# Zero-padded attention rows, more filler matmuls and separate PSUM banks in a fused pooled-attention and soft-MoE kernel

## The chip, the core and the metric

The kernel runs on one core of a Trainium2 chip. The time is what the device takes for one launch, in microseconds (us). It was measured in three runs: median 175.56 us, lowest 175.49, highest 175.78. A profiled execution of the same kernel gives the views that are quoted below. Its engines are PE (matmuls; PEld is the load of their stationary operand), DVE (vector), ACT (scalar), POOL (GpSimd, which here issues the loads) and SP (which issues the stores).

## The reference

Two stages are computed. The first is attention with keys and values that are means over eight neighbouring positions; the second mixes all tokens into 32 slots, runs four slots through each of eight experts, and mixes the slots back into the tokens.

```python
# batch 8, heads 8, seq 576, head_dim 64; pool = 8, so 72 keys and values
k_p = k.reshape(B, H, Sp, pool, D).mean(axis=3)
v_p = v.reshape(B, H, Sp, pool, D).mean(axis=3)
attn = softmax(scale * q @ k_p.T)
x = (attn @ v_p).transpose(0, 2, 1, 3).reshape(4608, 512)
logits = x @ phi                              # 4608 x 32
d = softmax(logits, axis=0)                   # over the tokens
slot_input = d.T @ x                          # 32 x 512, four rows for each expert
h = maximum(slot_input[e] @ w1[e], 0)         # 512 -> 1024, eight experts
slot_out[e] = h @ w2[e]                       # 1024 -> 512
c = softmax(logits, axis=1)                   # over the slots
out = c @ slot_out                            # 4608 x 512, float32
```

Inputs and outputs are float32. The kernel works in bf16; the loads convert on the way.

## The kernel before, in words

Batches are taken two at a time: four pairs. Within a pair there are two quarters `qd`, of four heads each and both batches. For each pair `prepare_kq` (L248) averages k by matmuls with `pmat` (L227), turns the means over (L243) and turns q over (L259). `prepare_v` (L270) does the same for v and multiplies by `iphi`, so that each row of `vp` holds 64 values of v and the 32 values of v times phi. A column of ones in `vp` (L154) makes the sum of the exponentials.

`score_unit` (L294) forms scores for one head: two matmuls with 64 contracted rows (L299) and one ACT exponential (L301) into `exa`, of which 72 partitions are used, one for each pooled key. `u_tile` (L304) takes the exponentials as the stationary operand and `vp` as the moving one (L314), 128 tokens at a time. DVE then takes the reciprocal of the sums (L319, tile `rec`, three buffers) and scales the result into `xs` (L325), or ACT does the scaling (L323). One quarter has nine u tiles; tiles 4 to 8 of a quarter are formed while the next quarter's scores are computed. Those of the very last quarter come behind the loop, in part in PSUM that the scores used (`spare`).

`combine` (L376) takes a finished pair: `weigh` (L328) sums the logits over the heads, on PE by default and for pair 1 on POOL (`ADDERS`), and exponentiates them to `ee`; `gather` (L346) multiplies `ee` with x into `G_ps`; `turn` (L358) turns `ee` over into `cT`. For the last pair this is written out behind the loop.

Then come the experts: `hidden` (L521) for the first layer, `second_layer` (L545) for the second, `row_sums` and `turn_sums` (L414, L423) for the sums of c. The last expert's second-layer weights arrive in two halves of columns, three pieces each (L499), in memory that the last pair frees late. `begin` (L622) starts the output of one half, and `tiles` and the last loop write the rest, 36 row tiles in all, stored by SP (L607).

`busy(n)` (L583) is a filler: a float32 matmul of n columns on data in `cT`, whose result nobody reads. A scheduler orders the instructions of PE, ACT, DVE and SP up to the end of the attention part; POOL's order is as written throughout, and behind the attention part the order of all engines is as written. Each engine runs its own row in that order, and waits on semaphores where an operand is not ready. The loads all go through one queue that POOL issues to, and they land in the order of issue.

Of the kernel before, what the change touches and what calls it, by code (L numbers as in the profile page):

```python
# [8 lines left out]
FP = mybir.dt.float32  # L9
BF = mybir.dt.bfloat16  # L10
# [8 lines left out]
def kernel(  # L19
# [10 lines left out]
    nc = tc.nc  # L30

    B, H, S, D = q.shape
    POOL = 8
    SP = S // POOL
# [15 lines left out]
    XW = D + NS  # L50
    HQ = H // 2
# [98 lines left out]
    nc.scalar.copy(out=big[:, 0, CUT // 2:CUT], in_=kf[:, CUT // 2:CUT])  # L150

    vp = [consts.tile([SP, H, XW + 2], BF, name=f"vp{i}") for i in range(5)]
    for t in vp:
        nc.vector.memset(t[:, :, XW:XW + 1], 1.0)  # L154
# [115 lines left out]
    def prepare_v(pair):  # L270
# [13 lines left out]
        for b in range(2):  # L284
            for qd in range(2):
                ps = ps_m.tile([SP, HQ, XW], FP, name="v_ps", tag="m")
                for hh in range(0, HQ, 2):
                    n = (qd * HQ + hh) // 2
                    nc.tensor.matmul(out=ps[:, hh:hh + 2], lhsT=vpar[:, b * HQ + n], rhs=iphi[:, n],
                                     start=True, stop=True)  # L290
                nc.scalar.copy(out=vp[(2 * pair + b) % 5][:, qd * HQ:(qd + 1) * HQ, 0:XW], in_=ps)
                yield
# [11 lines left out]
    def u_tile(pair, qd, t, ex, by_scalar=False, ps=None):  # L304
# [13 lines left out]
        rec = small.tile([128, HQ], FP, name="rec", bufs=3)  # L318
# [55 lines left out]
    ADDERS = {1: 2}  # L374
# [75 lines left out]
    last = None  # L450
    for pair in range(NP):
        for qd in range(2):
# [4 lines left out]
            ex = [exa[0:SP, (2 * pair + qd) % 2, b] for b in range(2)]  # L457
            for i in range(9):
                if i < 8:
                    score_unit(pair, i // 4 * H + qd * HQ + i % 4, ex[i // 4][:, i % 4])  # L460
# [120 lines left out]
    cTf = cT.rearrange("p r u -> p (r u)").bitcast(FP)  # L581

    def busy(n):  # L583
        nc.tensor.matmul(out=idle[:, 0:n], lhsT=cTf[:, 0:128], rhs=cTf[:, 0:n], start=True, stop=True)
# [80 lines left out]
    busy(512)  # L665
    turn_sums()
    busy(512)
    busy(512)
    for e in range(4, E - 2):
        second_layer(e)  # L670
    busy(512)
    second_layer(E - 2, 0, 5)
    busy(512)
    second_layer(E - 2, 5, FJ)
    second_layer(E - 1, 0, 3, 0)
    second_layer(E - 1, 3, J7, 0)
# [43 lines left out]
```

## Time and profile before

| what | value |
|---|---|
| runs: median, lowest, highest | 175.56, 175.49, 175.78 us |
| the profiled execution's own time | 175.54 us |
| its span, first to last instruction | 173.8 us |
| mean granted TensorE clock | 0.916 |
| busy: PE, DVE, ACT, POOL | 128.0, 93.0, 89.1, 21.7 us |
| loads through POOL's queue | 30.48 MB written, 85.5% of 16 DMA engines' span |
| stores and one load through SP's queue | 10.49 MB, 15.3% |
| loads last issued, at 138.71 us; first store issued | 147.31 us |

The profile gives the stretch, engine and line of each instruction. In a row of the order in time the first number is the start in us from the span's start, the second the length; in square brackets stands the idle time of the engine just before and what ended it. In a row of a stretch each engine's busy time is followed by its instructions in brackets; then come the granted clock (1.00 is full speed), the share of the 16 DMA engines, and GB/s. In a row of a group the number ahead of the bar is its busy time and the mean in ns. "72*128" ahead of a shape means 72 contracted rows and 128 columns of the stationary operand.

### The profile page before, as it was taken

Reading aid. Unit: us, or ns where it says so; the run is one execution under the profiler, and the core shown is the slowest. Engines: PE = TensorE matmul, PEld = TensorE weight load, DVE = VectorE, ACT = ScalarE, POOL = GpSimd, SP = SyncE. Lnnn points to the kernel's source line nnn. Section 1 sums busy time; section 2 is a strip of 40 time slices with the busy share of each in tenths; the row PEclk is TensorE's granted clock in tenths of the full one; section 3 lists DMA queues with packets and bytes.
Section 4 is the critical chain, followed back from the end, with each engine's and each line's share of the span. In section 5 each row is a group of like instructions: output and inputs, shape, how many; then the busy total and the mean of one; then the engine's idle time right before and its main releaser. Section 6 shows DMA issues by size and latency. Waiting matters only on the chain.

```text
span 173.8 us, 2847 instructions
## 1 busy us (share of the span) xinstructions
PE 128.0 (74%) x1104; PEld 69.0 (40%) x1104; DVE 93.0 (54%) x255; ACT 89.1 (51%) x171; POOL 21.7 (12%) x37
## 2 busy tenths in 40 slices
PE   0005787999899999999699999637999995897000
PEld 0002443665555665556444665422453322432000
DVE  5403344397868589786972856750542002799000
ACT  3201249885887739888490895463021103898000
POOL 7000111022100040009000104001410000000000
PEclk9999999999999999999957999955799999999555
DMA  5999999999999999999999999999999999999994
GB/s 192 247 216 223 216 216 212 220 214 212 218 218 214 215 219 214 218 215 214 215 219 211 223 211 219 213 221 211 223 211 219 208 197 177 301 390 447 404 453 183
DMA packets 8989, 41.13 MB, mean 237 GB/s; under 512 B 640, under 2 KB 4736, under 8 KB 5136
## 3 DMA queue, kind: packets, MB, share of 16 engines
q0 software_dynamic: 6080, 30.48, 85.5%
q1 hardware_dynamic: 2896, 10.49, 15.3%
q8 instruction: 8, 0.13, 0.3%
q14 instruction: 5, 0.04, 0.1%
HBM read 61.93 MB, written 9.44 MB: 411 GB/s over the span
## 4 chain that ended last, share of the span: by engine, by line
PE 40%; DMA 20%; ACT 16%; DVE 11%; issue 4%; POOL 1%; DVEq 0%; ACTq 0%; POOLq 0%
DMA xsa<-in_moe_w_dram 14%; PE pool_ps L227 9%; ACT exa L301 7%; DMA phi_f<-in_moe_phi_dram 7%; PE u_ps L314 6%; PE sc L299 6%; PE G_ps L349 4%; PE q_ps L259 4%; DVE w_sb L590 4%; DVE xsa L325 4%; PE lg_ps L342 2%; PE turn_ps L243 2%; ACT vmeans L233 2%; DVE rec L319 2%; PE f_ps L611 2%
## 5 line engine op out<-in xcount | busy, mean ns | idle before, releaser
L301 ACT ACTIVATE exa<-sc 72x576 bf16<-72x576 f32 x64 | 39.3, 653 | 6.6 <-PE u_ps L314 3.4
L325 DVE TENSOR_TENSOR xsa<-u_ps,rec 128x384 bf16<-128x384 f32 x66 | 35.8, 553 | 1.2
L314 PE MATMUL u_ps<-vp,exa 72*128 72x97 bf16 (+1 forms) x304 | 25.0, 215 | 4.6 <-DVE xsa L325 3.6
L314 PEld LDWEIGHTS <-exa 72*128 72x128 bf16 (+1 forms) x320 | 17.7, 103 | 15.6 <-DVE xsa L325 6.1
L299 PE MATMUL sc<-qTa,kp 64*72 64x288 bf16 x128 | 22.0, 313 | 1.6 <-ACT exa L301 1.0
L227 PE MATMUL pool_ps<-big,pmat 128*128 128x512 bf16 x64 | 17.5, 398 | 0.7 <-ACT qTa L263 0.6
L319 DVE RECIPROCAL rec<-u_ps 128x4 f32<-128x4 f32 x69 | 11.2, 174 | 11.5 <-PE u_ps L314 11.2
L179 PE MATMUL phi_ps<-spread,sel 128*128 128x256 bf16 x4 | 1.3, 394 | 15.1 <-DVE spread L174 15.1
L349 PE MATMUL G_ps<-xsa,ee 128*128 128x512 bf16 x36 | 11.5, 481 | 1.2 <-ACT ee L343 1.2
L259 PE MATMUL q_ps<-ident,big 128*128 128x128 bf16 x144 | 11.6, 219 | 0.8 <-DVE qTa L265 0.2
L299 PEld LDWEIGHTS <-kp 64*72 64x72 bf16 x128 | 7.9, 109 | 8.4 <-issue 3.0
L235 DVE TENSOR_REDUCE rsum<-rest_ps 128x64 f32<-128x512 f32 x8 | 5.5, 692 | 9.6 <-PE rest_ps L231 9.6
L265 DVE COPY qTa<-q_ps 128x768 bf16<-128x768 bf16 x16 | 8.7, 552 | 3.1 <-PE q_ps L259 3.0
L611 PE MATMUL f_ps<-so,cT 128*128 128x512 bf16 (+1 forms) x36 | 9.6, 353 | 0.7 <-ACT w_sb L588 0.6
L259 PEld LDWEIGHTS <-big 128*128 128x128 bf16 x144 | 8.6, 97 | 3.3 <-issue 1.8
L590 DVE TENSOR_SCALAR w_sb<-f_ps,recR 128x512 f32<-128x512 f32 x14 | 9.3, 741 | 0.1
L263 ACT COPY qTa<-q_ps 128x768 bf16<-128x768 bf16 x8 | 6.4, 795 | 5.7 <-PE q_ps L259 5.7
L590 DVE TENSOR_SCALAR exa<-f_ps,recR 128x256 f32<-128x256 f32 x8 | 3.8, 483 | 9.9 <-PE f_ps L633 9.6
L233 ACT CAST vmeans<-pool_ps 128x1024 bf16<-128x1024 f32 x4 | 4.0, 1012 | 9.2 <-PE pool_ps L227 9.2
L227 PEld LDWEIGHTS <-pmat 128*128 128x128 bf16 x64 | 5.9, 101 | 6.8 <-issue 2.1
L588 ACT ACTIVATE w_sb<-f_ps,recR 128x512 f32<-128x512 f32 x14 | 8.4, 696 | 0.2
L499 POOL DMA_DIRECT2D xsa<-in_moe_w_dram x6 | 4.1, 695 | 27.4 <-PE G_ps L349 13.2
(109 smaller groups left out, 160.9 us busy)
## 6 DMA issues: line engine op xcount, KB each, us to landing
w_sb<-in_moe_w_dram POOLq DMA_DIRECT2D x2, 3072.0 KB, 38.3
big<-in_q_dram POOLq DMA_DIRECT2D x4, 1152.0 KB, 12.8
big<-in_v_dram POOLq DMA_DIRECT2D x4, 1152.0 KB, 16.7
big<-in_moe_w_dram POOLq DMA_DIRECT2D x1, 4096.0 KB, 32.3
big<-in_k_dram POOLq DMA_DIRECT2D x3, 1152.0 KB, 21.4
out_dram<-w_sb SPq DMA_DIRECT2D x1, 3072.0 KB, 10.9
w_sb<-in_moe_w_dram POOLq DMA_DIRECT2D x2, 1024.0 KB, 19.6
qTa<-in_moe_w_dram POOLq DMA_DIRECT2D x1, 2048.0 KB, 33.2
```

Of the source, the lines that this page charges most:

```text
L227: nc.tensor.matmul(out=ps, lhsT=pmat, rhs=src[:, t:full * POOL:POOL, :], start=(t == 0), stop=(t == POOL - 1))
L259: nc.tensor.transpose(out=ps[:, t].rearrange("p n i -> p (n i)"), in_=q_sb[pair][:, tt:tt + 2, :].rearrange("p t d -> p (t d)"), identity= ...
L265: nc.vector.tensor_copy(out=dst, in_=ps)
L299: nc.tensor.matmul(out=ps[:, r, 0:S // 2], lhsT=kp[pair][rows, n], rhs=qT[pair][rows, n].rearrange("p t i -> p (t i)"), start=True, stop=True)
L301: nc.scalar.activation(out=dst.rearrange("p r (i t) -> p r i t", t=NU), in_=ps[:, :, 0:S // 2].rearrange("p r (t i) -> p r i t", i=NI), fu ...
L314: nc.tensor.matmul(out=ps[rows, hh], lhsT=ex[b][:, hh].rearrange("p r t -> p (r t)")[:, c:c + rows.stop - rows.start], rhs=vp[(2 * pair + ...
L319: nc.vector.reciprocal(out=rec, in_=ps[:, :, XW])
L325: nc.vector.tensor_tensor(out=dst, in0=ps[:, :, 0:XW], in1=rec.rearrange("p h -> p h ()").to_broadcast([128, HQ, XW]), op=ALU.mult)
L349: nc.tensor.matmul(out=ps, lhsT=ee[:, t].rearrange("p g s -> p (g s)"), rhs=x[:, t, :, 0:D], start=(t == 0), stop=(t == 8))
L588: nc.scalar.activation(out=dst, in_=src, func=AF.Copy, scale=by)
L590: nc.vector.tensor_scalar(out=dst, in0=src, scalar1=by, scalar2=None, op0=ALU.mult)
L611: nc.tensor.matmul(out=ps, lhsT=tokens(n), rhs=so[:, cols], start=True, stop=True)
```

## The change

Six things change.

- The tiles `vp` get 128 partitions instead of 72 and are zeroed by DVE first; partitions 64 to 127 of `exa` are zeroed too, once at the start. The u matmuls then contract 128 rows, 56 of them zero. The exponentials and the values are written to the first 72 as before.
- `rec` has eight buffers instead of three.
- Pair 0's logits are summed by DVE (`ADDERS` 0: 1), in one reduction over the heads, instead of by eight matmuls.
- Of the five last u tiles, those with i = 1 and 2 use the two `sc` tiles, one bank each; before, i = 2, 3 and 4 used three banks of them.
- Four fillers are added behind the last scores: 256 columns behind u tiles 1 and 4, 512 behind the logits, 256 behind the gather.
- In the expert part one more filler of 512 columns stands behind the row sums, and one of 256 ahead of each of the last expert's first two groups of slices.

```diff
+    nc.vector.memset(exa[64:128].rearrange("p n b h r t -> p (n b h r t)").bitcast(FP), 0.0)
-    vp = [consts.tile([SP, H, XW + 2], BF, name=f"vp{i}") for i in range(5)]
+    vp = [consts.tile([128, H, XW + 2], BF, name=f"vp{i}") for i in range(5)]
     for t in vp:
+        nc.vector.memset(t, 0.0)
         nc.vector.memset(t[:, :, XW:XW + 1], 1.0)
...
-        rec = small.tile([128, HQ], FP, name="rec", bufs=3)
+        rec = small.tile([128, HQ], FP, name="rec", bufs=8)
...
-    ADDERS = {1: 2}
+    ADDERS = {0: 1, 1: 2}
...
-            ex = [exa[0:SP, (2 * pair + qd) % 2, b] for b in range(2)]
+            ex = [exa[:, (2 * pair + qd) % 2, b] for b in range(2)]
...
-    spare = [wide[i // 2][:, i % 2, 0:HQ * (XW + 1)].rearrange("p (h c) -> p h c", h=HQ) for i in range(3)]
+    spare = [w[:, 0, 0:HQ * (XW + 1)].rearrange("p (h c) -> p h c", h=HQ) for w in wide]
...
     for i in range(5):
-        u_tile(*last[:2], 4 + i, last[2], by_scalar=i % 2 == 1, ps=spare[i - 2] if i >= 2 else None)
+        u_tile(*last[:2], 4 + i, last[2], by_scalar=i % 2 == 1, ps=spare[i - 1] if i in (1, 2) else None)
+        if i in (1, 4):
+            busy(256, G_ps)
     weigh(x, ee, 0, 9)
+    busy(512, G_ps)
     gather(x, G_ps, ee, 0, 9)
+    busy(256, wide[1][:, 1])
...
     row_sums()
-    busy(512)
+    busy(512, idle)
+    busy(512, idle)
     turn_sums()
...
     second_layer(E - 2, 5, FJ)
+    busy(256, idle)
     second_layer(E - 1, 0, 3, 0)
+    busy(256, idle)
     second_layer(E - 1, 3, J7, 0)
```

The scheduler places the first four fillers: on PE those of 256, 256 and 512 come among the last u tiles, and the fourth ahead of the second half of the last pair's logits. It also forms the last three score units of pair 3 behind pair 2's gather, where before they stood ahead of it. For pair 0's logits, DVE's row around the new reduction reads, before and now:

```order
L319 RECIPROCAL rec<-u_ps 128x4
L325 TENSOR_TENSOR xsa<-u_ps,rec 128x384
L319 RECIPROCAL rec<-u_ps 128x4 x2
L325 TENSOR_TENSOR xsa<-u_ps,rec 128x384
L265 COPY qTa<-q_ps 128x6x16x8
```

```order
L321 RECIPROCAL rec<-u_ps 128x4
L335 TENSOR_REDUCE hT<-xsa 128x9x32
L327 TENSOR_TENSOR xsa<-u_ps,rec 128x384
L321 RECIPROCAL rec<-u_ps 128x4
L267 COPY qTa<-q_ps 128x6x16x8
```

The reduction stands between a u tile's reciprocal and its scaling, ahead of a copy of q out of PSUM. The order on POOL and on SP is unchanged.

More of the change, by code (lines that the diff above doesn't have):

```diff
@@ L290, in prepare_v @@
                                      start=True, stop=True)
-                nc.scalar.copy(out=vp[(2 * pair + b) % 5][:, qd * HQ:(qd + 1) * HQ, 0:XW], in_=ps)
+                nc.scalar.copy(out=vp[(2 * pair + b) % 5][0:SP, qd * HQ:(qd + 1) * HQ, 0:XW], in_=ps)
                 yield
@@ L579 @@
     idle = ps_m.tile([128, 512], FP, name="idle_ps", tag="m")
-    cTf = cT.rearrange("p r u -> p (r u)").bitcast(FP)
-    def busy(n):
-        nc.tensor.matmul(out=idle[:, 0:n], lhsT=cTf[:, 0:128], rhs=cTf[:, 0:n], start=True, stop=True)
     def scaled(engine, dst, src, by):
@@ L664 @@
     row_sums()
-    busy(512)
+    busy(512, idle)
+    busy(512, idle)
     turn_sums()
-    busy(512)
-    busy(512)
+    busy(512, idle)
+    busy(512, idle)
     for e in range(4, E - 2):
         second_layer(e)
-    busy(512)
+    busy(512, idle)
     second_layer(E - 2, 0, 5)
-    busy(512)
+    busy(512, idle)
     second_layer(E - 2, 5, FJ)
+    busy(256, idle)
     second_layer(E - 1, 0, 3, 0)
+    busy(256, idle)
     second_layer(E - 1, 3, J7, 0)
```

5 lines of the change are left out of this document (4 added, 1 removed).

## The prediction

> **What bounds the kernel now.** I read first the stretches of time with the share of the DMA engines, then the chain of waits that ended last, then PE's and SP's order in time.
>
> ```profile
> core 0: us, PE busy (x) PEld busy (x) DVE busy (x) ACT busy (x) POOL busy (x), PEclk, DMA share, GB/s
> 4.00:112.00 108.00, 88.19 (x833) 52.31 (x834) 68.17 (x196) 66.69 (x123) 14.66 (x22) 0.97 1.03 218
> 112.00:124.00 12.00, 7.10 (x36) 3.17 (x33) 3.61 (x12) 5.04 (x17) 2.82 (x4) 0.57 1.03 216
> 141.00:146.50 5.50, 3.69 (x23) 1.18 (x21) 0.00 (x0) 0.47 (x1) 0.00 (x0) 1.00 1.36 193
> 147.00:147.50 0.50, 0.47 (x4) 0.27 (x3) 0.45 (x2) 0.48 (x2) 0.00 (x0) 1.00 0.84 112
> 147.50:148.00 0.50, 0.47 (x5) 0.20 (x4) 0.43 (x2) 0.50 (x2) 0.00 (x0) 1.00 0.39 50
> 148.00:148.50 0.50, 0.50 (x9) 0.22 (x6) 0.44 (x2) 0.43 (x2) 0.00 (x0) 1.00 0.54 178
> 148.50:172.00 23.50, 10.45 (x45) 4.28 (x41) 11.52 (x19) 11.27 (x21) 0.00 (x0) 0.78 1.00 398
> ```
>
> The next to last number of a row is the share of the 16 DMA engines. It is 1 or more from 4 us on, whether PE is busy (88 of 108 us) or half idle at a clock of 0.57 (112 to 124): the loads run at 216 to 218 GB/s through both. Then comes one dip, 147.0 to 148.5, and from there the stores fill the engines to the end. The dip costs (0.16 + 0.61 + 0.46) x 0.5 = 0.6 us. The kernel is one full stream of loads, a short hole, and one full stream of stores.
>
> ```profile
> 121.63 23.80 DMA xsa<-in_moe_w_dram
> 145.47 0.32 PE so_ps L549 x4
> 145.81 0.48 ACT so_a L588
> 146.33 0.28 PE f_ps L633
> 147.31 5.20 SPq L607 DMA_DIRECT2D out_dram<-exa  x8
> big<-in_k_dram POOLq DMA_DIRECT2D x1, 1152.0 KB, 21.4
> 4.06 0.55 POOL L100 DMA_DIRECT2D big<-in_k_dram  x1
> 19.48 0.53 POOL L100 DMA_DIRECT2D big<-in_q_dram  x1 [14.87 <-PE rest_ps L231]
> ```
>
> The second piece of the last expert's weights waits 23.8 us in that stream, lands at 145.43, and 1.9 us later SP issues the first store. Could late compute starve the loads? At 19.48 the load of the next q is issued while k of pair 1, issued at 4.06, lands only at 25.5: compute may slip by almost 6 us there. So 170 us of the time hang on transfers that this change does not touch. What is open is whether PE stands ready at 145.47, and how long the hole is.
>
> ```profile
> 137.56 1.98 PE L584 MATMUL idle_ps<-cT 128*128 128x512 f32 x4
> 143.18 0.40 PE L549 MATMUL so_ps<-xsa,hT 128*32 128x512 bf16 x3
> 144.18 0.29 PE L549 MATMUL so_ps<-xsa,hT 128*32 128x256 bf16 x3 [0.60 <-DMA xsa<-in_moe_w_dram]
> 145.47 0.29 PE L549 MATMUL so_ps<-xsa,hT 128*32 128x256 bf16 x4 [1.00 <-DMA xsa<-in_moe_w_dram]
> ```
>
> PE is early there: it idles 0.60 and 1.00 us for the last landings, at a granted clock of 1.00.
>
> **Part 1: fillers between the last landings.** Two fillers of 512 columns take 1.98 us as four matmuls, so one is 0.99 us and one of 256 columns about 0.50. Added: one of 512 behind the row sums, and one of 256 ahead of each of the last two waits. Here is PE's order from the filler ahead of expert 6's last slices to the second wait, before:
>
> ```order
> L584 MATMUL idle_ps<-cT 128x512
> L549 LDWEIGHTS hT
> L549 MATMUL so_ps<-xsa,hT 32x512
> L549 LDWEIGHTS hT
> L549 MATMUL so_ps<-xsa,hT 32x512
> L549 LDWEIGHTS hT
> L549 MATMUL so_ps<-xsa,hT 32x512
> L549 LDWEIGHTS hT
> L549 MATMUL so_ps<-xsa,hT 32x256
> ```
>
> and the same stretch now:
>
> ```order
> L560 MATMUL so_ps<-xsa,hT 32x512
> L495 MATMUL idle_ps<-cT 128x256
> L560 LDWEIGHTS hT
> L560 MATMUL so_ps<-xsa,hT 32x256
> L560 LDWEIGHTS hT
> L560 MATMUL so_ps<-xsa,hT 32x256
> L560 LDWEIGHTS hT
> L560 MATMUL so_ps<-xsa,hT 32x256
> L495 MATMUL idle_ps<-cT 128x256
> L560 LDWEIGHTS hT
> L560 MATMUL so_ps<-xsa,hT 32x256
> ```
>
> The fillers stand ahead of the matmuls that wait for the landings. Work added: 0.99 + 0.50 + 0.50 = 1.99 us; cover: 0.60 + 1.00 = 1.60 us. If PE comes to this stretch no earlier than before, it is late by 0.39 us at 145.47, and as everything behind is one chain to the first store, the end moves by all of it. If it comes earlier by X, the time is 175.54 + max(0, 0.39 - X). Of an X above 0.39 nothing is left, since the landing decides. The clock there is 1.00 already, so there is no gain to have. Now X, term by term.
>
> **Part 2: zero rows at the start (DVE).** Before and now, DVE from the cast of k on, or just ahead of it:
>
> ```order
> L158 MEMSET iphi 128x384
> L165 MEMSET sel 128x256
> L184 MEMSET siT 128x512
> L149 CAST big<-exa 128x1024
> L186 MEMSET hz 128x64
> ```
>
> ```order
> L149 CAST big<-exa 128x1024
> L156 MEMSET vp_103 128x8
> L156 MEMSET vp_104 128x8
> L155 MEMSET vp_105 128x392
> L151 MEMSET exa 64x4608
> L156 MEMSET vp_105 128x8
> L155 MEMSET vp_106 128x392
> L160 MEMSET iphi 128x384
> ```
>
> ```profile
> 1.02 0.91 DVE L125 MEMSET hT<- 128x1024 uint32 x1 [1.02 <-PEq L704]
> 2.35 0.38 DVE L158 MEMSET iphi<- 128x384 uint32 x1
> 14.64 1.43 DVE L174 TENSOR_TENSOR spread<-phi_f,head 128x256 bf16<-128x256 f32 x4 [6.85 <-DMA phi_f<-in_moe_phi_dram]
> ```
>
> iphi and sel move behind the cast; siT and hz move behind `spread`. A memset costs (0.91 - 0.38)/640 = 0.83 ns an element, so 4608 take about 3.9 us and 392 about 0.4. Behind the cast come 3.9 + 2 x 0.4 + 0.65 (iphi, sel) - 0.1 (hz) = 5.25 us into an idle time of 6.85 us that ends with the landing of phi. That cover leaves some 1.5 us: cost 0, at most about 1 if a memset this long ran at 1.4 ns.
>
> **Part 3: pair 0's logits from PE to DVE** (`ADDERS` 0: 1).
>
> ```profile
> 55.21 0.60 PE lg_ps L342 x4
> 56.73 0.60 PE lg_ps L342 x4
> L235 DVE TENSOR_REDUCE rsum<-rest_ps 128x64 f32<-128x512 f32 x8 | 5.5, 692 | 9.6 <-PE rest_ps L231 9.6
> 57.54 0.36 DVE L319 RECIPROCAL rec<-u_ps 128x4 f32<-128x4 f32 x2 [1.55 <-PE u_ps L314]
> ```
>
> PE loses eight matmuls on the chain, 1.2 us. DVE gets one reduction of 9 x 32 x 8 = 2304 elements; by the reduction of 512 in 692 ns, 3.1 us at most, about 2.5 with the start counted once. Queued behind it are `xsa` and `qTa` copies that free PSUM for PE. Where DVE's idle 1.55 us hides it, PE gains up to 1.2; where nothing does, compute loses 3.1 - 1.2 = 1.9. I take -1.0.
>
> **Part 4: zero rows in the u matmuls, and the clock at 86 us.**
>
> ```profile
> L314 PEld LDWEIGHTS <-exa 72*128 72x128 bf16 x256 | 15.6, 101 | 13.8 <-DVE xsa L325 5.4 <-issue 3.6 <-DVE rec L319 0.3
> L259 PEld LDWEIGHTS <-big 128*128 128x128 bf16 x144 | 8.6, 97 | 3.3 <-issue 1.8
> 86.39:89.81 3.42, 3.36 (x23) 1.61 (x24) 2.74 (x9) 3.17 (x6) 0.00 (x0) 0.50 1.03 216
> 89.81:93.22 3.41, 3.41 (x15) 1.56 (x16) 1.54 (x5) 1.68 (x3) 0.00 (x0) 0.50 1.02 214
> 86.45 0.51 PE L314 MATMUL u_ps<-vp,exa 72*128 72x97 bf16 x4 [0.31 <-DVE xsa L325]
> 90.87 2.62 PE L349 MATMUL G_ps<-xsa,ee 128*128 128x512 bf16 x6
> ```
>
> A weight load of 72 rows takes 101 ns and one of 128 rows 97: padding the rows costs PE nothing by itself. PE was busy 3.36 of 3.42 us and the clock stayed at 0.50; after the next stretch, with 128-row matmuls, it came back. The first held matmuls of 64 and 72 rows: a reading, not a proof, that active rows count. The change makes the 72 to 128. It could spare one half-speed stretch (1.7 us) or both (3.4), or none; I take +1.5. The Trainium skill ("TensorE: Matmul & The Clock Gate", Part 1) says that one sustained busy window of about 3.4 us releases the clock; by that the first stretch should have released it, and the trace disagrees. By that rule the rows do not matter, this term is 0 and X is 1.2 instead of 2.7, with the same time but less reserve.
>
> **Part 5: the last u tiles.**
>
> ```profile
> 105.22 2.12 PE L349 MATMUL G_ps<-xsa,ee 128*128 128x512 bf16 x9
> 119.61 4.02 PE L349 MATMUL G_ps<-xsa,ee 128*128 128x512 bf16 x9 [1.22 <-ACT ee L343]
> 111.14 0.66 PE L342 MATMUL lg_ps<-xsa,ident 128*128 128x288 bf16 x4
> 117.25 1.14 PE L342 MATMUL lg_ps<-xsa,ident 128*128 128x288 bf16 x4 [1.01 <-DVE xsa L325]
> 113.70:117.11 3.41, 0.99 (x8) 0.64 (x8) 2.10 (x7) 2.37 (x11) 0.00 (x0) 0.50 1.03 216
> ```
>
> The last gather takes 4.02 us at half clock against 2.12, the logits 1.14 against 0.66: 2.4 us, if the clock holds. The four fillers (3 x 256, 512) are 2.5 us of PE, in a stretch where it is idle 2.4 of 3.4 us; if none of it were hidden, nothing is gained, and with the clock lost besides, about -1. Banks of their own and eight `rec` buffers take waits of 0.3 to 1 us out, which I leave as the reserve against the fillers. I take +2.2.
>
> X = 0 - 1.0 + 1.5 + 2.2 = 2.7; its ends are -1.0 - 1.9 + 0 - 1.0 = -3.9 and 0 + 1.2 + 3.4 + 2.4 = 7.0. So 175.54 + 0 = 175.5 us. (175.54 is the profiled run: 173.8 of span and 1.74 around it; the median of the runs is 175.56.)
>
> **Rivals.**
> - *PE comes late* (slower). Parts 4 and 5 give nothing and DVE's reduction holds the PSUM copies: X = -1.0, the fillers ahead of the last landing do the rest, and the time is 175.54 + 1.39 = 176.9. It decides from X below 0.39, measurably from 0.04. For it: three fillers are written ahead of the wait on an in-order engine. Against: 2.7 us of X.
> - *The loads start late* (slower). Three memsets of `vp` now stand beside POOL's first issues, 3 x 0.4: up to +1.2 us on the whole stream, 176.7. The Trainium skill ("SBUF — State Buffer", Who interferes with whom) tells of descriptor writing that is held up by DVE operations in a two-port mode. Against: the memsets of iphi, sel and siT stood there before, and the issue at 4.06 took 0.55 us beside 0.53 for the one at 19.48.
> - *The hole closes* (faster). If an already busy PE brought the stores forward, at most the 0.6 us of the hole go: 174.9. Against: matmuls began 0.04 us behind the landing.
> - *Compute paces the end after all* (faster): 175.54 - 2.7 = 172.8. Against: the share of 1.03 while PE idled.
> - *The clock falls in the last tiles in spite of the fillers*: part 5 is worth 0, X = 0.5, and the time stays 175.5; this lies in the forecast.
>
> **How the numbers follow.** A measurement tells about 0.2% (0.35 us) from no change. Forecast 0.62; PE late 0.20; loads late 0.03; hole 0.10; compute paces 0.05. Of the forecast's share 0.04 goes to scatter, half to each side: faster 0.05 + 0.10 + 0.02 = 0.17, slower 0.20 + 0.03 + 0.02 = 0.25, same 0.58. The range runs from the closed hole, 174.9, to X = -1.0, 176.9; the likeliest case alone is 175.2 to 175.9.
>
> **What the next profile would show.** Right: the load of the last expert's second piece still lands near 145.4, `so_ps` follows within 0.1 us, the first store issues near 147.3; DVE idles 1 to 2 us ahead of `spread`; the gather of pair 3 takes near 2.1 us at a clock of 1.00. Wrong: `so_ps` starts well behind that landing with a filler just ahead of it (PE late); POOL's first issues take over 0.6 us (loads late); a DMA share below 1 anywhere ahead of 141 us (compute starves the stream); stores that begin clearly ahead of 147 us.

## The result and the profile after

The changed kernel takes 178.0 us (median of 22 runs, 175.57 to 178.95), the kernel before 175.92 us in the same comparison (22 runs, 175.49 to 177.25). The ratio is 1.007, 95% interval 1.0048 to 1.0092: slower by 0.7%. Ratios and intervals, here and below, leave out runs more than 1.5% above the fastest of their kernel; of the changed kernel these are nine, at 178.29 to 178.95 with granted clocks like those of the rest, and the median of its other 13 is 177.09. The forecast was 175.5, range 174.9 to 176.9. The profiled execution of the changed kernel took 177.43 us, its span 175.7, at a mean granted clock of 0.925.

First the stretches of the changed kernel, in the columns that the prediction explained:

```profile
core 0: us, PE busy (x) PEld busy (x) DVE busy (x) ACT busy (x) POOL busy (x), PEclk, DMA share, GB/s
4.00:112.00 108.00, 87.39 (x796) 51.87 (x796) 76.23 (x202) 66.11 (x122) 14.65 (x22) 0.95 1.03 218
112.00:124.00 12.00, 8.89 (x66) 4.32 (x65) 5.02 (x17) 5.29 (x18) 1.51 (x2) 0.78 1.03 215
141.00:146.50 5.50, 5.50 (x33) 1.62 (x31) 0.00 (x0) 0.00 (x0) 0.00 (x0) 1.00 1.36 194
147.50:149.00 1.50, 1.25 (x12) 0.63 (x9) 0.35 (x1) 0.94 (x3) 0.00 (x0) 1.00 0.17 24
```

The loads are as before: share 1.03 at 215 to 218 GB/s. Between 141 and 146.5 us PE is now busy all 5.50 us, where it had 3.69 before. The hole behind the loads has grown: in the 1.5 us from 147.5 the engines are 0.17 used.

Then PE's order in time in the changed kernel, ahead of the last landing, and SP's first stores:

```profile
137.85 1.90 PE L495 MATMUL idle_ps<-cT 128*128 128x512 f32 x4
139.68 0.41 PE L429 MATMUL RT_ps<-identf,sums 9*128 9x9 f32 x4
140.02 1.98 PE L495 MATMUL idle_ps<-cT 128*128 128x512 f32 x4
141.93 1.05 PE L560 MATMUL so_ps<-qTa,hT 128*32 128x512 bf16 x16
...
145.56 0.40 PE L560 MATMUL so_ps<-xsa,hT 128*32 128x512 bf16 x3
145.88 0.70 PE L495 MATMUL idle_ps<-cT 128*128 128x256 f32 x2
146.51 0.29 PE L560 MATMUL so_ps<-xsa,hT 128*32 128x256 bf16 x3
146.73 0.70 PE L495 MATMUL idle_ps<-cT 128*128 128x256 f32 x2
147.36 0.29 PE L560 MATMUL so_ps<-xsa,hT 128*32 128x256 bf16 x4
149.21 5.20 SPq L614 DMA_DIRECT2D out_dram<-exa  x8
```

The last expert's second piece lands at 145.46, as before. But `so_ps` for it starts at 147.36, with a filler just ahead of it and no bracket: PE does not wait, it is late by 1.9 us. The first store issues at 149.21 instead of 147.31, 1.90 us later, and the kernel takes 177.43 instead of 175.54, 1.89 us more. The chain of the changed kernel says the same:

```profile
PE 52%; DVE 17%; ACT 13%; DMA 7%; issue 3%; POOL 1%; DVEq 0%; ACTq 0%; POOLq 0%
```

Of the loads only that of phi is left on it; from there to the first store the end of this execution hangs on compute.

**Three rows fix the lateness.** `si_ps` (the slot inputs turned over, just behind the last gather) and `RT_ps` (the turned sums) stand on PE's row in both kernels. Before:

```profile
124.40 0.30 PE L505 MATMUL si_ps<-ident,Gb 32*128 32x32 bf16 x4 [0.21 <-DVE Gb L356]
137.22 0.41 PE L427 MATMUL RT_ps<-identf,sums 9*128 9x9 f32 x4
```

and after:

```profile
121.22 4.02 PE L351 MATMUL G_ps<-xsa,ee 128*128 128x512 bf16 x9 [1.22 <-ACT ee L345]
126.01 0.30 PE L516 MATMUL si_ps<-ident,Gb 32*128 32x32 bf16 x4 [0.21 <-DVE Gb L358]
```

From `si_ps` to `RT_ps` PE takes 12.82 us before and 13.67 after: the filler behind the row sums is 0.85. From `RT_ps` to that `so_ps` it is 7.68 us after. The experiments give 6.20 for a kernel without the two fillers of 256 (e1, below). So before, PE would have been ready at 137.22 + 6.20 = 143.42, 2.05 us ahead of the landing at 145.47; the three fillers cost 0.85 + 1.48 = 2.33 us, which alone makes PE 0.28 late; and the changed kernel comes to `si_ps` 1.61 us later. 0.28 + 1.61 = 1.89, which is what the time rose by.

The 1.61 is not what the change did to the attention part, though. The granted clock changes in steps of 3.41 us, on a grid that lies differently in each execution (its phase). Seven profiled executions, the kernel before and six of the experiments below, have the same attention part. The table orders them by the end of the half-speed stretch near 90 us; `RT_ps` is given where the fillers ahead of it are the same too.

| execution | half speed ends | `si_ps` | `RT_ps` |
|---|---|---|---|
| e8 | 93.00 | 124.20 | 137.01 |
| before | 93.22 | 124.40 | 137.22 |
| e2 | 94.02 | 125.69 | |
| e3 | 94.03 | 125.72 | |
| e12 | 94.48 | 126.08 | |
| e9 | 94.85 | 126.42 | 139.23 |
| e16 | 95.36 | 126.68 | |

The later the grid, the later `si_ps`: over a range of 2.48 us, with nothing changed ahead of it. In the changed kernel that stretch ends at 94.84 and the next at 125.56, in e9 at 94.85 and 125.57; of the seven, e9 is the one to compare with:

```profile
126.42 0.30 PE L505 MATMUL si_ps<-ident,Gb 32*128 32x32 bf16 x4 [0.39 <-DVE Gb L356]
```

Against it the changed kernel comes to `si_ps` 0.41 us earlier, and to `RT_ps` 139.23 - (139.68 - 0.85) = 0.40 earlier. e4, which has the changed attention part too, comes at 125.38 with the stretch ending at 94.11, 0.3 earlier than e2 and e3. So at equal phase the changed attention part gains 0.3 to 0.4 us. At e9's phase PE without the new fillers would be ready at 139.23 + 6.20 = 145.43, only 0.04 ahead of the landing, and the lateness of the changed kernel is 2.33 - 0.04 - 0.40 = 1.89: the fillers, and no cover.

### The profile page after: what moved, and what is told of

The parts are those of the page before. It is cut to its first block, busy times and chain, and to the rows that moved or that the text cites. A ratio compares the mean times of both kernels' runs of the same rounds, so it can differ in the third digit from the quotient of the medians.

```text
span 175.7 us, 2856 instructions
## 1 busy us (share of the span) xinstructions
PE 132.4 (75%) x1110; PEld 71.2 (41%) x1110; DVE 102.6 (58%) x262; ACT 88.7 (51%) x171; POOL 21.7 (12%) x37
## 4 chain that ended last, share of the span: by engine, by line
PE 52%; DVE 17%; ACT 13%; DMA 7%; issue 3%; POOL 1%; DVEq 0%; ACTq 0%; POOLq 0%
PE pool_ps L229 10%; PE G_ps L351 7%; DMA phi_f<-in_moe_phi_dram 7%; PE u_ps L316 5%; DVE xsa L327 4%; PE sc L301 4%; ACT exa L303 4%; DVE w_sb L597 4%; PE idle_ps L495 4%; PE q_ps L261 4%; PE so_ps L560 3%; DVE hT L335 2%; PE R_ps L420 2%; PE h_ps L539 2%; ACT vmeans L235 2%
## 5 line engine op out<-in xcount | busy, mean ns | idle before, releaser
L327 DVE TENSOR_TENSOR xsa<-u_ps,rec 128x384 bf16<-128x384 f32 x67 | 36.8, 555 | 1.5
L316 PE MATMUL u_ps<-vp,exa 128*128 128x97 bf16 (+1 forms) x312 | 24.5, 216 | 4.8 <-DVE xsa L327 3.5
L316 PEld LDWEIGHTS <-exa 128*128 128x128 bf16 (+1 forms) x320 | 17.8, 103 | 14.6 <-issue 4.5
L301 PE MATMUL sc<-qTa,kp 64*72 64x288 bf16 x128 | 20.7, 304 | 1.9 <-ACT exa L303 1.8
L229 PE MATMUL pool_ps<-big,pmat 128*128 128x512 bf16 x64 | 18.4, 417 | 0.7 <-ACT qTa L265 0.6
L351 PE MATMUL G_ps<-xsa,ee 128*128 128x512 bf16 x36 | 12.9, 519 | 1.3 <-ACT ee L345 1.2
L261 PE MATMUL q_ps<-ident,big 128*128 128x128 bf16 x144 | 12.1, 227 | 0.8 <-DVE qTa L267 0.3
L261 PEld LDWEIGHTS <-big 128*128 128x128 bf16 x144 | 9.1, 101 | 2.9 <-issue 1.7
L495 PE MATMUL idle_ps<-cT 128*128 128x512 f32 (+1 forms) x16 | 7.5, 573 | 0.0
```

Source lines behind the costliest of these rows:

```text
L229: nc.tensor.matmul(out=ps, lhsT=pmat, rhs=src[:, t:full * POOL:POOL, :], start=(t == 0), stop=(t == POOL - 1))
L261: nc.tensor.transpose(out=ps[:, t].rearrange("p n i -> p (n i)"), in_=q_sb[pair][:, tt:tt + 2, :].rearrange("p t d -> p (t d)"), identity= ...
L301: nc.tensor.matmul(out=ps[:, r, 0:S // 2], lhsT=kp[pair][rows, n], rhs=qT[pair][rows, n].rearrange("p t i -> p (t i)"), start=True, stop=True)
L316: nc.tensor.matmul(out=ps[rows, hh], lhsT=ex[b][:, hh].rearrange("p r t -> p (r t)")[:, c:c + rows.stop - rows.start], rhs=vp[(2 * pair + ...
L327: nc.vector.tensor_tensor(out=dst, in0=ps[:, :, 0:XW], in1=rec.rearrange("p h -> p h ()").to_broadcast([128, HQ, XW]), op=ALU.mult)
L351: nc.tensor.matmul(out=ps, lhsT=ee[:, t].rearrange("p g s -> p (g s)"), rhs=x[:, t, :, 0:D], start=(t == 0), stop=(t == 8))
```

## The experiments

Medians are of all runs of a kernel, and a difference to the changed kernel is given to both of its medians, 178.0 and 177.09; ratios are to the kernel before on the same chip. The medians of the kernel before in these comparisons lie between 175.63 and 175.92.

**e1: the changed kernel without the three late fillers.**

```diff
 row_sums()
 busy(512, idle)
-busy(512, idle)
...
-busy(256, idle)
 second_layer(E - 1, 0, 3, 0)
-busy(256, idle)
 second_layer(E - 1, 3, J7, 0)
```

> The changed kernel without the three new fillers of the expert part (part 1 undone, the rest kept). Theory A, PE comes late: in the changed kernel's profile the matmuls for the landing at 145.46 start at 147.36, 1.90 late, and 1.99 us of filler are taken away, so they would start at 145.4 to 145.5 and the time falls from 178.0 to about 176.0, within 0.3 of the kernel before. Theory B, the attention part's changes are what costs, by a way of their own (DMA, padded matmuls, the clock): the time stays near 178.

175.62 us (175.56 to 177.2); ratio 1.0004 [0.9982, 1.0027]. All that the change had cost is gone: 2.4 us from 178.0, 1.5 from 177.09. PE's order in e1:

```profile
139.97 0.41 PE L429 MATMUL RT_ps<-identf,sums 9*128 9x9 f32 x4
145.85 0.61 PE L560 MATMUL so_ps<-xsa,hT 128*32 128x512 bf16 x10
146.40 0.39 PE L637 MATMUL f_ps<-xsa,zT 128*128 128x256 bf16 x2
```

`f_ps` behind the last group comes 6.43 us after `RT_ps`; in the changed kernel it was 147.59 - 139.68 = 7.91. The two fillers of 256 cost 1.48, and so the last group stood at 7.68 - 1.48 = 6.20. In this execution PE was 0.70 late (139.97 + 6.20 - 145.47), and the time was 176.21, which is 175.54 + 0.67.

**e2: the kernel before with the three late fillers.** The same three lines, added to before.

> The kernel before with only the three new fillers of the expert part (part 1 alone). Theory A: PE has 1.99 us more ahead of the last landing; a run like the profiled one (1.60 us of idle) loses 0.4, a median run of before (175.92, already 0.4 above its fastest) loses the whole 2.0, so 176.0 to 177.9 with a wide scatter. Theory B: fillers stand in idle time and cost nothing, 175.9.

177.52 us (177.09 to 178.88); ratio 1.0097 [1.0061, 1.0134]. They cost as much in the kernel before. In its trace the rule of the three rows holds:

```profile
139.36 0.41 PE L427 MATMUL RT_ps<-identf,sums 9*128 9x9 f32 x4
147.04 0.29 PE L549 MATMUL so_ps<-xsa,hT 128*32 128x256 bf16 x4
```

147.04 is 139.36 + 7.68; 1.57 us behind the landing; 175.54 + 1.57 = 177.11, measured 177.09. But `RT_ps` stands 2.14 later than in the profiled execution of before, and the added filler is only 0.85 of it. The rest is the phase of the clock: the two executions stand in different rows of the table above.

**e3 and e4: before and after with no fillers at all in the expert part.** All `busy` lines from the row sums on are left out (five before, eight after).

> The kernel before without any filler in the expert part (five of 512 columns, about 5 us of PE, left out). Theory A: PE then waits at every landing, the time is the loads plus the stores, 175.5 in every run with a scatter under 0.2 us, where before went from 175.49 to 177.25. Theory C, the fillers are needed to hold the clock for the tail: a granted clock of 0.50 behind 145 us, the first store 0.3 to 1 us later, 175.9 to 176.6 in every run.

> The changed kernel without any filler in the expert part. Theory A: 175.5 as well, since a compute part that is 1.6 us later than before is still some 5 us ahead of the last landing. Theory B: near 178. Theory C: 175.9 to 176.6.

176.41 us (176.3 to 178.3), ratio 1.0044 [1.0019, 1.0068], and 176.71 us (176.19 to 177.91), ratio 1.0061 [1.0035, 1.0088]. So the fillers that stood there before are worth something. PE is in time in both profiled executions (`so_ps` at 145.62 and 145.48), but without fillers the clock falls to half behind the row sums and stays there while the output starts; e3, in one row:

```profile
138.41:155.47 17.06, 14.22 (x74) 5.68 (x75) 5.25 (x12) 6.77 (x14) 0.54 (x1) 0.50 0.99 210
```

Fillers pull in two directions here: they hold the clock for the output, and they stand ahead of a matmul that a landing releases.

**e5: the changed kernel with pair 0's logits on PE again.**

```diff
-    ADDERS = {0: 1, 1: 2}
+    ADDERS = {1: 2}
```

> The changed kernel with pair 0's logits on PE again (part 3 undone). The changed kernel is late in nearly every run, so its time reads X off directly: each us of compute that is saved ahead of the fillers is a us of time. If DVE's reduction costs compute the 1.0 us of the prediction: 177.0 (from 178.0). If it costs all that pair 1's stage lost in the trace (2.3 us more lag at 67 us than at 52): 175.7. If that lag is made good again by 94 us, as the trace's gather of pair 1 suggests: 178.

176.12 us (175.71 to 178.84); ratio 1.0036 [1.0002, 1.007]. That is 1.9 us below 178.0 and 1.0 below 177.09, though all late fillers are in. The intervals of the two kernels overlap, so the runs alone do not fix what DVE's sums cost; the traces show it. First DVE and PE of the changed kernel, around the sums for pair 0 (L335), and a stretch of PE's clock:

```profile
56.07 4.06 DVE L335 TENSOR_REDUCE hT<-xsa 128x288 f32<-128x2304 bf16 x1
60.03 0.56 DVE L327 TENSOR_TENSOR xsa<-u_ps,rec 128x384 bf16<-128x384 f32 x1
60.65 0.47 PE L316 MATMUL u_ps<-vp,exa 128*128 128x97 bf16 x4 [1.27 <-DVE xsa L327]
```

```profile
57.29:60.70 3.41, 1.63 (x20) 1.04 (x19) 3.41 (x4) 3.37 (x7) 0.00 (x0) 1.00 1.04 219
60.70:64.11 3.41, 3.35 (x27) 2.59 (x27) 3.07 (x9) 1.43 (x2) 0.83 (x2) 0.50 1.03 214
```

and the same stretches in e5:

```profile
57.29:60.70 3.41, 3.39 (x37) 2.15 (x35) 2.20 (x6) 2.50 (x4) 0.00 (x0) 1.00 1.03 217
60.70:64.11 3.41, 3.41 (x36) 2.16 (x35) 2.41 (x7) 1.34 (x2) 1.29 (x3) 1.00 1.01 211
```

The reduction takes 4.06 us. The scaling of `xsa` stands behind it, PE waits for the bank, is busy 1.63 of 3.41 us, and the next stretch is granted half the clock. All five profiled kernels with these sums (the changed one, e1, e4, e6, e7) show such a half-speed stretch of 3.41 us between 60 and 65.5 us; none of those without the sums does (e11 apart, see there). By pair 2's gather only 0.7 us of it are left (106.27 against 105.56). Behind it the order differs: in the five kernels with the sums the scheduler forms the last three score units of pair 3 behind that gather, in e5 ahead of it, as before. The last exponentials of pair 3, after and then e5:

```profile
109.76 1.17 ACT L303 ACTIVATE exa<-sc 72x576 bf16<-72x576 f32 x2
111.60 0.65 ACT L303 ACTIVATE exa<-sc 72x576 bf16<-72x576 f32 x1
```

```profile
105.41 1.17 ACT L303 ACTIVATE exa<-sc 72x576 bf16<-72x576 f32 x2
118.87 2.12 PE L351 MATMUL G_ps<-xsa,ee 128*128 128x512 bf16 x9 [1.22 <-ACT ee L345]
145.53 0.29 PE L560 MATMUL so_ps<-xsa,hT 128*32 128x256 bf16 x4 [0.38 <-DMA xsa<-in_moe_w_dram]
```

In e5 the clock is 1.00 from 93.78 us to 162, the last gather takes 2.12 us, and PE waits for the landing in spite of all fillers. Its profiled execution took 177.46 us all the same, for another reason. Its row of the store of 2048 KB, with the time from issue to landing at the end:

```profile
out_dram<-w_sb SPq DMA_DIRECT2D x1, 2048.0 KB, 9.7
```

Before, this was 7.6. The last store, issued behind it, then landed 1.9 us later than before.

**e6: the changed kernel without the zero rows.** `vp` has 72 partitions again, the memsets go, and the u tiles contract 72 rows.

> The changed kernel with 72 rows in the u matmuls again and no memsets for them (parts 2 and 4 undone). If zero rows gain clock, as part 4 of the prediction had it (+1.5 us of X): 179.5. If they do nothing and the start costs nothing: 178.0. If the start is what makes compute late by 0.7 us from the first pair on: 177.3.

178.02 us (176.19 to 178.64); ratio 1.0102 [1.0057, 1.0147], an interval that overlaps that of the kernel with them. e13 and e18 below show the clock with and without.

**e7: the changed kernel without the four fillers among the last u tiles.**

> The changed kernel without the four fillers among the last u tiles. If they hold the clock there (part 5, +2.2 us of X): slower, up to 180. If the clock falls at the last gather with them too, as in the profiled run, they only stand in the way: up to 2.5 us of PE less, 176 to 177.5.

176.83 us (175.7 to 178.8); ratio 1.0039 [1.0011, 1.0067]. That is 1.2 us below 178.0 but 0.3 below 177.09, and the intervals overlap: a gain from the fillers is not seen, a cost not shown. The changed kernel's own row at 121.22 has the gather at 4.02 us, half speed, though the fillers ran. e6 has the fillers and e7 has not, at nearly the same phase (half speed ends at 96.10 and 95.92): `si_ps` stands at 127.21 and 125.48, but the next half-speed stretch ends at 126.82 and 130.06, and `RT_ps` stands at 140.88 and 141.05. Beside the sums the fillers are worth nothing by then.

**e8 and e9: the kernel before with other late fillers.** e8 leaves out one filler of 512 behind the turned sums; e9 also adds the two of 256.

> The kernel before with one of its five fillers of 512 columns less (the second behind the turned sums). Theory A: one more us of room at the last landing, so the runs of before that are late (up to 177.2) come down, median 175.5 and scatter under 0.5 us, if the four left still hold the clock. If they do not: 176.3, as without any filler.

> The kernel before with one 512-column filler behind the turned sums left out, and one filler of 256 columns ahead of each of the last expert's first two slice groups: the amount of filler work ahead of the last landing stays as before, only half of it moves into the waits. Theory 1 (what counts is the amount of PE work ahead of the last landing against PE's spare time there): so_ps starts within 0.1 us of the landing near 145.45 in a run of common clock phase, first store near 147.3, time 175.5 to 175.7. Rival (a filler directly ahead of a waiting matmul costs by its place): so_ps 0.3 to 0.5 us behind the landing, 175.9 to 176.1.

e8: 175.54 us (175.42 to 177.01), 0.9978 [0.9951, 1.0005]. e9: 175.84 us (175.52 to 176.48), 0.9987 [0.9964, 1.0009]. Neither is measurably other than before. e9's profiled execution was late (`RT_ps` 139.23, `so_ps` 146.06, 0.59 behind the landing, time 176.12): six of its twelve runs lie at 175.52 to 175.58 and six at 176.1 to 176.5. So the amount of work ahead of the landing counts; that the fillers now stand in the waits does not save them. e8's profiled execution shows the opposite failure, a clock at half from the first stores on, and took 177.01:

```profile
147.62:154.44 6.82, 6.77 (x30) 2.85 (x29) 3.92 (x9) 5.18 (x11) 0.00 (x0) 0.50 0.80 265
```

**e10: the changed kernel without DVE's sums and with two fillers of 512 less** (one behind the row sums, one behind the turned sums).

> The changed kernel without the vector engine's sums for pair 0, and with one 512-column filler instead of two behind the row sums and one instead of two behind the turned sums: it keeps the fillers in the last tiles, which gave the last gather at full clock (2.12 us), and has 1.0 us less filler work ahead of the last landing than the kernel without those sums had. Theory 1 (two causes added up: the sums, and the amount of late filler work): never late at the landing, 175.4 to 175.6, with fewer single runs above 177 than the 4 of 12 without the sums alone. Rival (the scatter of that run came from the stores and not from lateness): median 175.7 to 176.2 and again a third of the runs above 177.

175.56 us (175.47 to 176.76); 0.9981 [0.9952, 1.001]. Eight of twelve runs lie between 175.47 and 175.58, none above 176.8. This is the best version of the change that I found, level with the kernel before; that it beats it is not shown.

**e11 and e18: the changed kernel without DVE's sums and without the four fillers among the last u tiles.**

> The changed kernel without the vector engine's sums for pair 0 and without the four fillers in the last tiles. Theory 1 (without the sums the four fillers hold the clock and so gain the 1.9 us of the last gather, which pays for the three late ones): taking them out puts the last gather back to 4.0 us at half clock, so_ps comes 0.4 us or more late, and the time goes up from 176.1 to that of the kernel before with the late fillers alone, 177.0 to 177.5. Rival (the four fillers are only PE work, and the phase of the clock decides whether it falls): the time stays at 176.1 or falls to 175.7.

> The changed kernel without the vector engine's sums and without the fillers in the last tiles, once more. Theory 1 (zero rows lift some stretches of the u tiles over what the clock gate asks for, at some phases): again 175.5 to 175.7 with over half of the runs below 175.6, and less time at a granted clock of 0.50 between 110 and 128 us than the 13.65 us of the kernel without zero rows. Rival (the earlier run was the chip's or the phase's chance): 176.3 to 176.8 like the kernel without zero rows, and the same 13.65 us.

e11: 175.58 us, ratio 0.9998 [0.9969, 1.0027]; its profiled execution took 211.51 us at a granted clock of 0.59 and is not compared with the others. e18, the same kernel on another chip: 176.02 us (175.45 to 176.91), 0.9995 [0.9964, 1.0026]. That is far from the 177.0 to 177.5 that I had expected of e11. It put the question what pays for the late fillers here and not in e2.

**e13, e14, e15: the kernel before with the late fillers, and with the new banks and eight `rec` buffers, the banks alone, `rec` alone.**

```diff
-spare = [wide[i // 2][:, i % 2, 0:HQ * (XW + 1)]... for i in range(3)]
+spare = [w[:, 0, 0:HQ * (XW + 1)]... for w in wide]
-... ps=spare[i - 2] if i >= 2 else None)
+... ps=spare[i - 1] if i in (1, 2) else None)
-rec = small.tile([128, HQ], FP, name="rec", bufs=3)
+rec = small.tile([128, HQ], FP, name="rec", bufs=8)
```

> The kernel before with the three late fillers, the new banks of the last u tiles and eight rec buffers; no zero rows, no sums by the vector engine, no fillers in the last tiles. Theory 1 (banks and rec end the waits of 0.9 us ahead of the last u tiles, which brings the last gather 1.0 to 1.5 us forward): last logits near 118 instead of 119.3 at the same clock phase, so_ps on the landing, 175.5 to 175.7. Rival (the zero rows paid, or the earlier run was chance): 177.0 to 177.5 as with the late fillers alone.

> The kernel before with the three late fillers and the new banks alone. If the waits of 0.94 and 0.93 us ahead of the last u tiles are waits for a PSUM bank to come free, the banks alone give the whole gain, 175.5 to 175.8. If they are waits for one of the three rec buffers or for the normalizing copies themselves, the time stays at 177.0 to 177.5.

> The kernel before with the three late fillers and eight rec buffers alone. Theory 1 says that the banks pay: 177.0 to 177.5, unchanged. Rival: the rec buffers pay, 175.5 to 175.8.

e13: 176.59 us (176.03 to 179.15), 1.0048 [1.0016, 1.0081]. e14: 176.68 us (176.09 to 179.03), 1.0049 [1.0016, 1.0082]. e15: 177.79 us (175.62 to 178.21), 1.0086 [1.0051, 1.012]. Against 177.52 with the late fillers alone, the banks are worth about 0.9 us by the medians and `rec` nothing, though the intervals overlap. The traces are clearer: from the first to the second half of the last pair's logits (`lg_ps`) PE takes 6.74 us in e2 and 5.97 in e15, without the new banks, and 5.66 in e14 and 4.96 in e13, with them; by the nearest phases (e2 and e14, e15 and e13) they gain 1.0 to 1.1 us there. By the median e13 is half of what I expected, and the trace has the reason: its `si_ps` stands at 123.50, 2.2 us ahead of e2's 125.69, but the clock is at half until 127.98, while in e2 it returns at 124.74. From `si_ps` to `RT_ps` e13 needs 15.53 us instead of 13.67; of the 2.2 us gained, 1.9 are given back.

e13 and e18 differ in the zero rows alone (and in names), and their profiled executions happen to have the same phase of the clock. A stretch around 87 us and the last u tiles, e13 with 72 rows:

```profile
87.02:90.43 3.41, 3.33 (x24) 1.53 (x21) 2.51 (x7) 3.16 (x6) 0.00 (x0) 0.50 1.07 226
90.43:93.85 3.42, 3.42 (x14) 1.45 (x13) 1.48 (x4) 1.38 (x3) 0.00 (x0) 0.50 1.01 211
114.33:127.98 13.65, 11.22 (x75) 4.97 (x79) 4.55 (x13) 3.38 (x11) 2.83 (x4) 0.50 1.04 218
```

and e18 with 128:

```profile
87.02:90.43 3.41, 3.32 (x22) 1.50 (x21) 2.35 (x7) 3.17 (x5) 0.00 (x0) 0.50 1.06 221
90.43:93.85 3.42, 3.42 (x12) 1.41 (x13) 1.48 (x4) 1.22 (x3) 0.00 (x0) 0.50 1.06 220
114.33:127.98 13.65, 11.33 (x75) 5.00 (x79) 4.43 (x12) 3.26 (x11) 2.82 (x4) 0.50 1.04 218
```

The clock is the same in every stretch, and so is the time, 176.76 and 176.72. At this phase of the clock zero rows are worth nothing. e1 and e6, which up to `si_ps` differ in the zero rows alone, are a pair at another phase (half speed ends at 96.14 and 96.10): `si_ps` stands at 127.17 and 127.21. Why the medians of e13 (176.59) and of e11 and e18 (175.58 and 176.02) lie apart on different chips stays open.

**e12, e16, e17: the kernel before with its late fillers on 32 rows, on 128 rows, and on 128 rows of which 96 hold zeros.** Each float32 filler becomes four bf16 matmuls of 512 columns:

```diff
-nc.tensor.matmul(out=idle[:, 0:n], lhsT=cTf[:, 0:128], rhs=cTf[:, 0:n], start=True, stop=True)
+for _ in range(4):
+    nc.tensor.matmul(out=idle[:, 0:n], lhsT=cT[0:32, 0, 0:128], rhs=cT[0:32, 0, 0:n], start=True, stop=True)
```

e16 has `cT[0:128, ...]` instead; e17 a tile of zeros into whose first 32 rows those of `cT` are copied.

> The kernel before with each late filler (one fp32 matmul of 512 columns on 128 rows) written as four bf16 matmuls of 512 columns on 32 rows: the same time of PE, a quarter of the rows in use. Reading of the prediction's part 4 (rows in use count for the clock): the granted clock falls to 0.50 between 138 and 146 as it does where there are no fillers at all, and the time is about 176.4. Rival (only the time in which PE runs counts): the clock stays 1.00 from 130 us to 147 us, and the time is that of the kernel before, 175.5 to 175.9.

> The kernel before with each late filler written as four bf16 matmuls of 512 columns on all 128 rows. Reading that the rows in use count: the clock stays at 1.00 from 125 to 147 us, so_ps on the landing, 175.5 to 176.2. Rival (bf16 against fp32 is what made the clock fall with 32 rows): the clock falls to 0.50 behind 139 us again and the time is 180 to 182.

> The kernel before with each late filler written as four bf16 matmuls of 512 columns on 128 rows, of which rows 32 to 127 hold zeros in both operands; rows 0 to 31 hold the same values as in the run with 32 rows. Theory 1 (the rows that a matmul spans count, whatever they hold): the clock holds at 1.00 from 128 to 147 us as with 128 rows of data, time 175.5 to 176.3. Rival (rows of zeros do not count, so that the padding of part 4 could not work): the clock falls to 0.50 behind 138 us as with 32 rows, time 180 to 182.

e12: 181.39 us (two runs), ratio 1.0305 [1.024, 1.037]. e16: 176.06 us (175.46 to 177.23), 1.0009 [0.9972, 1.0046]. e17: 176.25 us (175.5 to 177.5), 1.0014 [0.9975, 1.0052]. In e12:

```profile
135.44:138.85 3.41, 3.41 (x9) 0.72 (x8) 0.00 (x0) 0.57 (x1) 0.10 (x1) 1.00 1.02 211
138.85:142.26 3.41, 3.41 (x13) 1.43 (x12) 0.39 (x2) 0.00 (x0) 0.44 (x1) 0.50 1.07 202
142.26:145.68 3.42, 3.42 (x21) 0.89 (x20) 0.00 (x0) 0.00 (x0) 0.00 (x0) 0.50 1.42 192
```

In e17:

```profile
138.00:142.00 4.00, 4.00 (x26) 1.51 (x28) 0.40 (x2) 0.57 (x1) 0.54 (x1) 1.00 1.07 208
142.00:146.00 4.00, 4.00 (x41) 1.38 (x34) 0.00 (x0) 0.14 (x1) 0.00 (x0) 1.00 1.42 193
```

With 32 rows PE is busy without a pause and the clock falls to 0.50 and stays there for 13.65 us. With 128 rows it holds, and it holds as well where 96 of the rows are zeros. (The moment of the fall also depends on the phase. That full stretches of 32-row fillers do not bring the clock back is the stronger sign: behind the gather with 128 rows, the row of e13 at 90.43, it comes back.) So the rows that a matmul spans count, whatever they hold.

**The rule of the three rows, over all kernels with the late fillers.** "Late" is `so_ps` less the landing at 145.47; times are of the profiled executions.

| kernel | `RT_ps` | `so_ps` | difference | late | 175.54 + late | measured |
|---|---|---|---|---|---|---|
| changed | 139.68 | 147.36 | 7.68 | 1.89 | 177.43 | 177.43 |
| e2 | 139.36 | 147.04 | 7.68 | 1.57 | 177.11 | 177.09 |
| e6 | 140.88 | 148.56 | 7.68 | 3.09 | 178.63 | 178.64 |
| e7 | 141.05 | 148.74 | 7.69 | 3.27 | 178.81 | 178.80 |
| e13 | 139.03 | 146.71 | 7.68 | 1.24 | 176.78 | 176.76 |
| e14 | 138.36 | 146.05 | 7.69 | 0.58 | 176.12 | 176.09 |
| e15 | 138.23 | 145.91 | 7.68 | 0.44 | 175.98 | 175.97 |
| e18 | 138.97 | 146.65 | 7.68 | 1.18 | 176.72 | 176.72 |
| e5 | 136.32 | 145.53 | waits | 0.06 | 175.60 | 177.46 |

Eight of nine agree to 0.03 us. In these executions the lateness at this one matmul is the whole effect; e5 is the store stream told of above.

## Why the prediction was wrong

**What bounds the kernel** was right: one load stream, a hole, the store stream. The landings did not move, the DMA share stayed at 1.03, and compute counts only where it is late at the last landing. The mechanism that decides, time = 175.54 + max(0, 0.39 - X), was right as well: against the profiled execution of before X is -1.61, which gives 177.54, and 177.43 was measured. Two of its terms failed. The first is the cover in part 1: the 1.60 us of idle in one execution were taken as the kernel's. In e2 nothing is changed ahead of the fillers, so X is 0 but for the phase; the sum then gives 175.93, and the median is 177.52. The second is the sum for X, given as +2.7: at equal phase it is +0.3 to +0.4. Of the -1.61, about 2.0 us are the phase (`RT_ps` at 139.23 in e9, 137.22 in before). The rival *PE comes late*, which had 0.20, is what happened, but only in part by its reason: it took X as -1.0 and the cover as given, and it was the cover that was missing.

**Part 1, late fillers.** 1.99 us of work against 1.60 of cover, 0.39 late: measured 2.33 against 2.05, 0.28 late. Each size was off by a sixth to a quarter, and the difference was near. Not seen was how much the cover depends on the execution. Before's profiled execution has `RT_ps` at 137.22; e9, whose work is the same up to that point, has it at 139.23, when the clock's 3.41 us stretches fall otherwise. There 139.23 + 6.20 = 145.43: the cover of 2.05 us is down to 0.04, and the three new fillers cost their whole 2.3 us. Without them e1 is level with before. One profiled execution was taken as the kernel; of the seven in the table only one was more favourable.

**Part 2, zero rows at the start,** cost 0: right, and in the main for the reason given, with nothing to spare. The memset of 4608 elements took what was estimated:

```profile
8.12 3.90 DVE L151 MEMSET exa<- 64x4608 f32 x1 [1.02 <-issue]
14.61 1.43 DVE L176 TENSOR_TENSOR spread<-phi_f,head 128x256 bf16<-128x256 f32 x4
```

`spread` starts at 14.61, before 14.64. But DVE has no idle time ahead of it any more, where 1.5 us were expected: the queue was late with single items (an idle of 1.02 us for which the profile shows no releaser), and the cover just sufficed.

**Part 3, DVE's sums: -1.0, measured about -2.3 where they run and -2.2 at `RT_ps`; -1.0 to -1.9 in the time (e5).** The reduction took 4.06 us, more than the 3.1 that the prediction set as its upper bound from a reduction over another layout. What the bound left out is what a wait of PE does to the clock: 3.41 us at half speed followed, some 1.7 us more. `rest_ps` for pair 2's v came 3.1 us later, of which 0.7 were there at 51 us, so that 2.3 are left; before and then after:

```profile
64.59 0.38 PE L231 MATMUL rest_ps<-big,pmat 128*128 128x512 bf16 x1
```

```profile
67.66 0.38 PE L233 MATMUL rest_ps<-big,pmat 128*128 128x512 bf16 x1
```

The later stages made most of it good on PE (the gather of pair 1 started 0.5 us earlier than before). Behind pair 2's gather the last exponentials come 5 us late, by the scheduler's order as well as by the delay; no run separates the two. e10, without the sums, has nearly the phase of the changed kernel (half speed ends at 95.03 and 94.84) and one filler less ahead of `RT_ps`: 139.68 - 0.85 - 136.67 = 2.2 us.

**Part 4, zero rows and the clock: +1.5, measured 0.** The reading that the rows in use count was right (e12 against e16 and e17). The step from it to a gain failed: the matmuls that were padded have 97 columns and share their stretch with the scores, which keep 64 rows; the clock stays at 0.50 in the same stretch (e13, e18). That padding them changes too little of the stretch is my reading; no run pads the scores. The prediction weighed this against the Trainium skill ("TensorE: Matmul & The Clock Gate", Part 1), by whose rule the term would be 0. The rule gave the right sum, though not by its reason: that section says that the clock is set by how busy PE has been, and e12 shows PE busy 3.41 of 3.41 us at 0.50.

**Part 5, the last tiles: +2.2, measured about 0 for the fillers in the changed kernel (e6 against e7).** The gather ran at half clock, 4.02 us as before. That the fillers can hold the clock is shown in e5 (2.12 us) and partly in e10: `si_ps` stands at 121.76 in e5 and at 123.39 in e18, without them, at nearly the same phase (half speed ends at 93.78 and 93.84), a gain of 1.6 us. They did not hold it in any profiled kernel with DVE's sums, where the last exponentials come behind pair 2's gather; the prediction added the two terms as if they were independent. The rival *the clock falls in the last tiles in spite of the fillers* had X = 0.5, since it took the fillers themselves as hidden. They are not: from the end of pair 2's gather to the last logits PE needs 9.3 us in e5 with the fillers and 8.5 in e18 without. The banks, left as a reserve, were worth about 1 us (e13, e14). Banks 1.0, fillers 1.6 and sums -2.2 (a price that includes the fillers' lost gain) add up to the 0.4 of equal phase; the pairs are of different phases, so part of this agreement may be chance.

**The range** ended at 176.9, from X = -1.0. The ends of X were given as -3.9 and 7.0; the lower one would have set the upper end at 175.54 + 4.3 = 179.8, and the measured median lies in between. The text had this number and did not let it into the range.

## What to carry to other kernels

A filler on an in-order engine ahead of a matmul that a landing releases is paid in full as soon as the engine is late: find the last row ahead of the wait whose distance to it is fixed, and compare it with the landing over several executions, not one. Compare two kernels' traces only at the same phase of the clock. Price an operation that moves to another engine with what queues behind it, with what the resulting wait does to the TensorE clock and with the order that the scheduler then chooses, and don't add gains that depend on the same stretch. A reserve read from one profile is worth no more than the spread of the clock's phase leaves of it.

## What the runs showed of the hardware

- The clock of TensorE is granted in stretches of 3.41 us (or their multiples) whose grid is not tied to the program's start: the first that the traces record at full speed began between 17.91 and 24.46 us. In seven executions of one and the same work `si_ps` moved by 2.48 us with it. The Trainium skill ("TensorE: Matmul & The Clock Gate", Part 1) calls the window free-running, and these traces agree. Single runs of the kernel before go from 175.49 to 177.25 us; how much of that is the phase is not shown, since they have no trace.
- Fillers of 32 rows held nothing: PE was busy 13.62 of 13.65 us at a clock of 0.50 (e12). Rows of zeros counted like rows of data (e17).
- Work that comes earlier into a half-speed stretch gains little: e13 was 2.2 us earlier at `si_ps` and 0.3 us at `RT_ps`.
- The same chain of stores can take 1.9 us longer with nothing late ahead of it (e5: 2048 KB landing after 9.7 us instead of 7.6); no run here shows why.
